# A delta-rule scan and a gated MLP on one core: another order of pieces and lags with fewer idle products, and 64-row products of two neighbouring first-layer tiles in the two halves of the array

## The chip, the core and the metric

The program runs on one core of a Trainium2 chip. Its time is the device time of one execution in microseconds (us); several executions are taken and their median counts. Engines are named as in the profile: PE (TensorE, products), PEld (its weight loads), DVE (VectorE), ACT (ScalarE), POOL (GpSimd) and SP (the engine that issues the transfers).

## The reference

Two parts follow each other. The first is a recurrence over 768 steps for 4 batches x 8 heads with a state of 40x40; the second is a gated MLP with spatial gating on the 4 x 768 x 320 array that the first part leaves.

```python
for t in range(S):                      # S = 768, D = 40
    y[:, :, t] = einsum('bhd,bhde->bhe', rt, state)
    Sa = einsum('bhde,bhe->bhd', state, at)
    state = state * wt[:, :, None, :] - einsum('bhd,bhe->bhde', Sa, bt) + einsum('bhd,bhe->bhde', vt, kt)

h = gelu(x @ w_in)                      # x: 4 x 768 x 320, w_in: 320 x 1024, tanh form
u, v = h[..., :512], h[..., 512:]
v_n = (v - mean) / sqrt(var + 1e-6) * g_ln
v_s = einsum('ts,bsd->btd', w_sg, v_n) + b_sg[None, :, None]    # w_sg: 768 x 768
out = x + (u * v_s) @ w_out             # w_out: 512 x 320
```

All is float32. The large products are made of rounded halves: a value is split into a rounded high part and a rounded rest (names ending in h and l), and a product of two values is high x high, high x low and low x high.

## The kernel before

**The scan.** The 768 steps are 12 chunks of 64. For each chunk DVE builds the gates, PE makes the products ab inside the chunk, ACT copies their blocks out (nts, kbt), POOL inverts a triangular block by pairs of steps tg and x, and PE carries the state from chunk to chunk (ru, sp, ut, pq, yp in the trace). ACT also fills the constant zeros of the tiles rt, vut and xt at the start, by copies from a zeroed tile warm. The results go to DRAM through xd and come back as the rows of x (xt).

**The MLP.** The work of a batch is cut into pieces. x0 and x1 split the two halves of x into the tiles xh and xl (split_x, line 1084). v0 to v5 are the v half of the first layer for 128 rows each (in_v, line 1114; trace name hv, 8 products of 512 columns). u0 to u7 are the u half, transposed, 128 columns by 384 rows each (in_u, line 1142; hu, 8 products of 384 columns). s0 to s7 are the gating product with w_sg (sg, 18 products: 6 chunks of 128 rows times 3 of high and low), o0 to o5 the last layer (op). A batch's first layer has a depth of 320: two chunks of 128 rows and a third of 64. The 64-row tail of x is loaded twice, into both halves of a 128-row tile. In xh[:, 2] the upper half holds the high part and the lower half the rest, so that one 128-row product with the high weights wih[:, 2] does for both; in the product with the low weights wil[:, 2] only the 64 rows of the high part are wanted.

**Order.** The order of the pieces is a table: SEQ0 for batch 0 with batch 1's first layer between (line 93), SEQ for later batches (line 91), SEQL for the last one. run (line 1281) goes through it; before each piece it issues the weight preparation that is due there (loads, splits of w_sg at positions SGS into wsh and wsl, splits of w_out at OUTS; SGE and OUTE say which engine subtracts, V for DVE and G for POOL). Behind each piece product (line 1096) puts the piece's ACT, DVE and POOL steps on a list with a lag in pieces (later), and tick issues what is due: for a v piece p, q, q, v, the statistics bs and mv, the root rs on POOL, and the split into vh (ACT) and vl (POOL). The first five pieces of batch 0 (FILL) run inside the scan.

The scan's order is set by tables of due times and lags too (CH, GPOS, LAG and others); a list JUNK of (due time, count) puts idle products of 512 columns on PE, whose results nobody reads, and a piece "j6" is six of them. All instructions of an engine run in the order in which the program issues them; every row of the trace names line 157, the helper that records them, and so the pieces are told by their tiles.

Of the kernel before, what the change touches and what calls it, by code (L numbers as in the profile page):

```python
# [35 lines left out]
EW = 1.24  # L36
WARM = (14, 0)
T0 = 7.27
T1 = 16.98
T2 = 3.25  # L40
TX = 17.74
LX = 2.88
YM = 64
HEAT = ((13.17, 11),)
LV = 7.67
C1 = 15.05
WP = 16.2
W16 = 0.27
K16 = 0
TB0 = 1.08  # L50
TB1 = 14.03
CUT0 = (2,)
HALF = 9
ROWS0 = (0, 26)
T3 = 11.21
T4 = 15.34
CH = ((0.45, 2.04, 5.42, 6.21, 1.13, 7.18, 8.59, 11.36, 3.3, 10.06, 13.31, 14.77), (0.21, 1.37, 6.72, 4.0, 8.34,
    5.6, 9.88, 10.86, 3.24, 6.16, 13.32, 13.76))
GPOS = (((0.01, 0.33, 0.61, 1.31, 3.87, 4.25, 4.26, 4.27, 0.611), (2.52, 2.51, 2.79, 3.49, 5.81, 6.43, 6.44, 6.45,
# [5 lines left out]
GE = ("VVVVV", "VVV", "V", "V")  # L65
START = (13.53, 0.06)
E0A = "GGGG"
E0K = "GVGG"
E1A = "GGGG"
E1K = "GGGV"  # L70
BACK = (17.21, 22.21, 30.49, 23.63)
GX = (24.18, 3.53)
CG = 0.7978845608028654
G1 = 0.044715
ENDS = {(9, 1): (("g", 0.01),), (10, 1): (("r", 0.01),), (11, 0): (("i", 5.0),)}
PIN = 266.02
DSTEP = ((-13.06, -3.36, 0.0, 0.13, 3.41, 3.62), (-16.79, -1.11, 0.0, 0.61, 3.02, 3.47))
DEC = ((275.89, 0), (276.24, 0), (284.23, 0), (286.85, 0), (290.7, 1), (297.59, 1), (298.13, 1), (306.35, 0),
    (309.82, 0), (317.07, 1), (323.45, 0), (329.7, 1))
PX = 266.05  # L80
PV = 294.03
PL = 335.9
FILL = (("x0", 0, 319.86), ("v0", 0, 331.35), ("v1", 0, 344.98), ("v2", 0, 346.14), ("u0", 0, 349.9))
AFTER = {"v": (0.56, 0.57, 1.47, 1.57, 2.13, 2.48, 2.96, 4.17, 5.19), "u": (1.14, 1.97, 2.82, 3.17), "x": ()}
PX1 = 0
EARLY = 4
PSG = 313.1
SGD = (-6.74, -0.32, 1.37)
SGA = ()
VRING = 10  # L90
SEQ = ("x0", "s1", "x1", "s2", "s0", "s3", "s4", "v0", "s5", "v1", "o0", "o1", "o2", "s6", "s7", "v2", "u0", "v3",
    "u1", "v4", "v5", "o3", "o5", "o4", "u2", "u3", "u4", "u5", "u7", "u6")
SEQ0 = (("x0", 0), ("v0", 0), ("v1", 0), ("v2", 0), ("u0", 0), ("u3", 0), ("x1", 0), ("u1", 0), ("u2", 0), ("v3",
# [4 lines left out]
XL = 4  # L98
REST = 9
SGS = (3, 6, 4, 5, 11, 10, 10, 13, 13, 13, 14, 14)  # L100
OUTS = (11, 12, 12, 14, 15, 18, 19, 18)
XE = "VVVVVVVVVVVV"
UE = "VVVVVVVV"
OSTEP = (-3, -1, 0, 0, 0, 0)
SGE = "GGGGGVGVVVVV"
OUTE = "VVGGGGGG"
SECOND = (17.86, 0.35)
ZERO = (-1, 12.11)
LAST = 2
IS = 1  # L110
NS = 0
PQ = 1
MK = 40
JUNK = ((294.28, 5), (295.93, 4), (307.25, 6), (312.36, 3), (312.43, 1), (346.91, 3), (349.9, 4))
TP = 1
UT = 0
GL = (0.53, 0.99)
LAG = ((0.48, 1.44, 5.43, 0.01, 4.92, 1.62, (0.04, 0.48, 0.01, 1.02), (1.56, 1.57, 0.55, 1.09), 1.82, 0.23, 0.77,
    0.11), (0.2, 0.01, 3.21, 0.78, 1.1, 0.64, (0.26, 0.27, 0.89, 0.9), (0.01, 0.02, 2.06, 2.07), 0.01, 3.4, 0.06,
    0.01))  # L120
# [50 lines left out]
def attention(tc, a, xd, flag, keep, ps, mlp=None):  # L171
# [4 lines left out]
    with ExitStack() as ctx:  # L176
# [643 lines left out]
        def both(c, n, at, w, nm="tv"):  # L820
# [64 lines left out]
class Mlp:  # L885
# [198 lines left out]
    def split_x(self, b, n):  # L1084
        t, h, l = self.xts[b % 2, n], self.xh, self.xl
        self.xin[n] = b
        c = slice(384 * n, 384 * n + 384)
        for k in range(2):
            self.split(h[:, k, c], l[:, k, c], t[:, k], self.A, self.pick(XE, 6 * b + 3 * n + k))
        self.A.copy(out=h[:, 2, c], in_=t[:, 2])  # L1090
        self.pick(XE, 6 * b + 3 * n + 2).tensor_tensor(out=h[64:128, 2, c], in0=t[64:128, 2], in1=h[64:128, 2, c].bitcast(F32), op=ALU.subtract)

    def pick(self, s, k):
        return self.G if k < len(s) and s[k] == "G" else self.V

    def product(self, ops, *steps):
        for i, (o, l, r) in enumerate(ops):
            self.T.matmul(o, lhsT=l, rhs=r, start=(i == 0), stop=(i == len(ops) - 1), skip_group_check=True)
        if self.hold is not None:
            self.hold += [f for _, _, f in sorted(steps, key=lambda x: x[:2])]  # L1100
            return
        self.later(*steps)
        self.tick()
# [10 lines left out]
    def in_v(self, b, tt):  # L1114
        V, G, sb = self.V, self.G, self.pv
        xh, xl, wih, wil = self.xh, self.xl, self.wih, self.wil
        c, f = slice(128 * tt, 128 * tt + 128), slice(HF, DF)
        ops = [(xh[:, k, c], x[:, k, f]) for x in (wih, wil) for k in range(3)]
# [12 lines left out]
        def halves():  # L1131
            h, l = pair
            self.split(h, l, v)
            self.vn[b, tt] = h, l

        self.product([(o, *x) for x in ops], *self.gelu2(o, HF, v),
                     (1, 7, lambda: V.bn_stats(out=bs, in_=v)), (1, 8, lambda: V.bn_aggr(out=mv, in_=bs)), (1, 9, root),
                     (2, 7.5, lambda: V.tensor_scalar(out=v, in0=v, scalar1=mv[:, 0:1], scalar2=rs,
                                                    op0=ALU.subtract, op1=ALU.mult)),
                     (2, 10, halves))  # L1140

    def in_u(self, b, f, n):
# [138 lines left out]
    def run(self, ahead, verdict=None):  # L1281

        done = [(x, b) for x, b, _ in FILL] if ahead else []
        seq, jobs = [], []
# [12 lines left out]
        seq = [x for x in seq if x[1] < B and x not in done and (ahead or x[0][0] != "j")]  # L1297
# [134 lines left out]
```

## Time and profile before

| what | us |
|---|---|
| runs of the kernel before | 619.60, 621.16, 621.56 |
| median | 621.16 |
| the profiled execution | 620.27 |
| its span, first to last instruction | 618.5 |
| PE busy | 578.4 (94%) |
| DVE, ACT, POOL busy | 487.2, 390.9, 374.3 |

The profiled execution is one execution; its span leaves out 1.8 us around the first and last instruction. Mean granted clock of TensorE over the span: 0.945 of full speed. Busy shares are averages over stages that have little in common, the scan up to about 350 us and the MLP after it.

### The profile page before, as it was taken

What the parts mean: (1) busy time and instruction counts of PE and PEld (TensorE: products, weight loads), DVE (VectorE), ACT (ScalarE), POOL (GpSimd) and SP (SyncE); (2) the same over time, 40 slices, a digit from 0 to 9 for tenths busy, and PEclk for the clock granted to TensorE, in tenths of its full rate; (3) what the DMA queues carried; (4) which work ended last, traced back from release to release, by engine and by line L of the source; (5) the groups of instructions that cost most, each with busy time, mean ns of one, the idle gap of its engine ahead of it and who ended that gap; (6) DMA issues with size and microseconds to landing.
All of it is one profiled execution on the core that took longest, in us unless ns stands there. A gap on an engine that the chain in (4) does not pass through costs nothing.

```text
span 618.5 us, 24511 instructions
## 1 busy us (share of the span) xinstructions
PE 578.4 (94%) x10060; PEld 520.8 (84%) x10060; DVE 487.2 (79%) x1085; ACT 390.9 (63%) x1113; POOL 374.3 (61%) x842
## 2 busy tenths in 40 slices
PE   5758999999999999999979999699999999999996
PEld 5557888888888888888868789699899989999995
DVE  7867798988889897798787988898887779568732
ACT  6938798988979889788764856544544256224410
POOL 7768688888888888888886425445533332343230
PEclk9555899999999999999989999899999999999999
DMA  6513243454434543433433424420111103010002
GB/s 207 168 41 89 76 123 104 121 129 117 113 106 117 132 120 104 116 100 92 140 92 100 129 78 141 141 65 10 33 55 54 34 1 108 1 34 13 20 1 70
DMA packets 56889, 54.06 MB, mean 87 GB/s; under 512 B 35840, under 2 KB 47360, under 8 KB 56768
## 3 DMA queue, kind: packets, MB, share of 16 engines
q1 hardware_dynamic: 56768, 52.40, 29.9%
q8 instruction: 81, 1.33, 0.9%
q14 instruction: 40, 0.33, 0.2%
HBM read 44.52 MB, written 7.86 MB: 85 GB/s over the span
## 4 chain that ended last, share of the span: by engine, by line
PE 50%; DVE 15%; ACT 14%; POOL 9%; issue 6%; DMA 4%; SPq 1%; POOLq 0%; ACTq 0%; DVEq 0%
PE sg L157 13%; PE op L157 6%; PE hu L157 6%; PE hv L157 6%; POOL x L157 5%; POOL tg L157 4%; PE ab L157 4%; ACT nts L157 3%; PE sp L157 3%; PE yp L157 3%; PE ru L157 2%; DVE at L157 2%; DMA main<-main 2%; DVE sc L157 2%; DVE ex L157 2%
## 5 line engine op out<-in xcount | busy, mean ns | idle before, releaser
L157 POOL TENSOR_TENSOR tg<-x,n 128x126 f32<-128x126 f32 (+24 forms) x334 | 123.1, 369 | 34.2 <-ACT x L157 5.5
L157 POOL TENSOR_TENSOR x<-x,tg 128x126 f32<-128x126 f32 (+24 forms) x334 | 126.3, 378 | 26.1
L157 PE MATMUL sg<-wsh,vh 128*128 128x384 f32 x192 | 66.0, 344 | 5.7 <-ACT wsh L157 4.5
L157 POOL TENSOR_TENSOR gx<-g,gy 128x384 fp32r<-128x384 f32 x30 | 31.7, 1061 | 64.6 <-ACT gy L157 64.6
L157 PE MATMUL sg<-wsl,vh 128*128 128x384 f32 x192 | 65.7, 342 | 0.4 <-POOL wsl L157 0.4
L157 PE MATMUL sg<-wsh,vl 128*128 128x384 f32 x192 | 65.7, 342 | 0.0
L157 ACT ACTIVATE nts<-ab 32x256 f32<-32x256 f32 x192 | 62.0, 323 | 5.7 <-DVE at L157 3.1
L157 PE MATMUL pq<-rt,vut 128*64 128x128 f32 x768 | 52.9, 281 | 0.0
L157 ACT CAST gy<-g 128x384 fp32r<-128x384 f32 x30 | 15.4, 514 | 55.5 <-DVE g L157 52.2
L157 PE MATMUL ab<-at,kb 64*64 64x64 f32 x1536 | 38.5, 242 | 11.0 <-POOL kb L157 5.4
L157 ACT CAST vh<-v 128x512 fp32r<-128x512 f32 x24 | 14.9, 621 | 51.6 <-DVE v L157 51.6
L157 PE MATMUL yp<-pqs,kbt 128*64 128x64 f32 x768 | 46.5, 225 | 1.0 <-ACT kbt L157 0.4
L157 PEld LDWEIGHTS ab<-at,kb 64*64 64x64 f32 x1536 | 31.7, 150 | 16.6 <-POOL kb L157 6.0
L157 POOL TENSOR_TENSOR vl<-v,vh 128x512 fp32r<-128x512 f32 x24 | 31.6, 1317 | 20.9 <-ACT vh L157 20.9
L157 PEld LDWEIGHTS pq<-rt,vut 128*64 128x64 f32 x768 | 41.8, 139 | 2.3 <-issue 0.7
L157 PEld LDWEIGHTS sg<-wsh,vh 128*128 128x128 f32 x192 | 36.9, 192 | 6.6 <-ACT wsh L157 4.8
L157 PE MATMUL yp<-rt,s 80*40 80x64 f32 x704 | 42.3, 219 | 0.0
L157 PEld LDWEIGHTS yp<-pqs,kbt 128*64 128x64 f32 x768 | 37.1, 136 | 5.4 <-DVE sc L157 2.2
L157 DVE SCALAR_TENSOR_TENSOR g<-sg,gl,bt 128x384 f32<-128x384 f32 x32 | 19.7, 615 | 25.4 <-PE sg L157 24.4
L157 DVE TENSOR_TENSOR at<-ab,mask 64x256 f32<-64x256 f32 x96 | 35.7, 407 | 4.5 <-PE ab L157 3.9
L157 PEld LDWEIGHTS sg<-wsl,vh 128*128 128x128 f32 x192 | 36.9, 192 | 1.0 <-POOL wsl L157 0.8
L157 PE MATMUL ru<-rhsb,xt 64*64 64x40 f32 x768 | 32.2, 234 | 5.7 <-ACT xt L157 5.3
(166 smaller groups left out, 1652.7 us busy)
## 6 DMA issues: line engine op xcount, KB each, us to landing
main<-main SPq DMA_DIRECT2D x88, 160.8 KB
vs<-vb SPq DMA_DIRECT2D x24, 160.0 KB
vu<-vs SPq DMA_DIRECT2D x24, 160.0 KB
rt<-rt SPq DMA_DIRECT2D x48, 80.0 KB
vut<-vt SPq DMA_DIRECT2D x24, 160.0 KB
xd<-yt SPq DMA_DIRECT2D x96, 40.0 KB
xt<-xd SPq DMA_DIRECT2D x16, 192.0 KB
out<-y SPq DMA_DIRECT2D x16, 192.0 KB
```

Of the source, the lines that this page charges most:

```text
L157: return self.tc.keep_in_program_order(f(*a, **k))
```

## The change

Four things are changed.

1. The product with the 64 useful rows becomes the last of a v or u piece. Where two u or v pieces are neighbours in the table, the first piece leaves it out, and behind the second piece's other products both follow as 64-row products: the first piece's on rows 0 to 63 of xh, the second's on rows 64 to 127 of a new tile xb, which holds the high part there. The follow-up steps of both pieces are then issued one after the other. A u or v piece without such a neighbour keeps its 128-row product. There are 23 such pairs (10 of two u pieces, 6 of two v, 7 of one each); 6 pieces of the tables stay alone, and so do those inside the scan. For xb, split_x makes two ACT casts of 64 rows out of one of 128. EARLY gives one pair of v tiles less to the scan's time, which makes room for xb.
2. The idle products in JUNK go from 26 to 13 and those in pieces from 6 (j6) to 5 (j2, j3).
3. The order of pieces: batch 0 now has u1 u2, v5 v4, v3 u5, u4, j2, u7 u6, s1; later batches have v0 and v1 side by side. One w_sg split is two positions earlier, one is subtracted on DVE instead of POOL, and pieces of w_out move.
4. The scan's due times and lags. On PE the scan's order stays as it was but for the idle products; on ACT copies of constants change place at the start.

```diff
-T1 = 16.98
+T1 = 17.63
...
-EARLY = 4
+EARLY = 3
...
-SEQ = ("x0", "s1", "x1", "s2", "s0", "s3", "s4", "v0", "s5", "v1", "o0", "o1", "o2", "s6", "s7", "v2", "u0", "v3",
+SEQ = ("x0", "s1", "x1", "s2", "s0", "s3", "s4", "v0", "v1", "s5", "o0", "o1", "o2", "s6", "s7", "v2", "u0", "v3",
...
-SGS = (3, 6, 4, 5, 11, 10, 10, 13, 13, 13, 14, 14)
+SGS = (3, 6, 4, 5, 11, 10, 10, 11, 13, 13, 14, 14)
-SGE = "GGGGGVGVVVVV"
+SGE = "GGGVGVGVVVVV"
...
-JUNK = ((294.28, 5), (295.93, 4), (307.25, 6), (312.36, 3), (312.43, 1), (346.91, 3), (349.9, 4))
+JUNK = ((296.7, 4), (299.18, 4), (312.36, 3), (314.34, 2))
...
+        self.pair, self.first = 0, None
...
+        self.xb = p.tile([128, S], F32R, name="xb")
...
     def split_x(self, b, n):
...
-        self.A.copy(out=h[:, 2, c], in_=t[:, 2])
-        self.pick(XE, 6 * b + 3 * n + 2).tensor_tensor(out=h[64:128, 2, c], in0=t[64:128, 2], in1=h[64:128, 2, c].bitcast(F32), op=ALU.subtract)
+        z = self.xb[64:128, c]
+        self.A.copy(out=z, in_=t[64:128, 2])
+        self.A.copy(out=h[0:64, 2, c], in_=t[0:64, 2])
+        self.pick(XE, 6 * b + 3 * n + 2).tensor_tensor(out=h[64:128, 2, c], in0=t[64:128, 2], in1=z.bitcast(F32), op=ALU.subtract)
...
-    def product(self, ops, *steps):
-        for i, (o, l, r) in enumerate(ops):
-            self.T.matmul(o, lhsT=l, rhs=r, start=(i == 0), stop=(i == len(ops) - 1), skip_group_check=True)
+    def product(self, ops, *steps, third=None):
+        ops = [(*x, not i, i == len(ops) - 1 and not third) for i, x in enumerate(ops)]
+        if third and not self.pair:
+            ops.append((*third(slice(0, 128)), False, True))
+        if third and self.pair == 2:
+            for k, f in enumerate((self.first[0], third)):
+                ops.append((*f(slice(64 * k, 64 * k + 64)), False, True))
+        for o, l, r, start, stop in ops:
+            self.T.matmul(o, lhsT=l, rhs=r, start=start, stop=stop, skip_group_check=True)
+        if third and self.pair == 1:
+            self.first = third, steps
+            return
+        if third and self.pair == 2:
+            self.later(*self.first[1])
+            self.tick()
...
     def in_u(self, b, f, n):
...
-        ops = [(x[:, k, fc], xh[:, k, c]) for x in (wih, wil) for k in range(3)]
+        ops = [(x[:, k, fc], xh[:, k, c]) for x in (wih, wil) for k in range(3 if x is wih else 2)]
...
-        self.product([(o, *x) for x in ops], *self.gelu2(o, 384, u))
+
+        def third(r):
+            return o, wil[r, 2, fc], (self.xb[r, c] if r.start else xh[r, 2, c])
+
+        self.product([(o, *x) for x in ops], *self.gelu2(o, 384, u), third=third)
...
     def run(self, ahead, verdict=None):
...
+            if self.pair == 1:
+                self.pair = 2
+            else:
+                self.pair = int(x[0] in "uv" and i + 1 < len(seq) and seq[i + 1][0][0] in "uv")
             self.piece(x, b)
```

The remaining lines of the diff are other numbers of these tables, and in_v has the same edit as in_u.

**PE, from the last u pieces of batch 0 to the start of s1** (hu and hv are the first layer's products, xl and wil low parts, idle the idle products, sg the gating product). Before:

```order
L157 MATMUL hu<-xh,wih 128x384 x3
L157 MATMUL hu<-xh,wil 128x384 x3
L157 MATMUL hu<-xl,wih 128x384 x2
L157 MATMUL hu<-xh,wih 128x384 x3
L157 MATMUL hu<-xh,wil 128x384 x3
L157 MATMUL hu<-xl,wih 128x384 x2
L157 MATMUL idle<-wih 128x512 x6
L157 MATMUL sg<-wsh,vh_7684 128x384
```

and now, from the end of the piece u4:

```order
L157 MATMUL hu<-xh,wil 128x384
L157 MATMUL idle<-wih 128x512 x2
L157 MATMUL hu<-xh,wih 128x384 x3
L157 MATMUL hu<-xh,wil 128x384 x2
L157 MATMUL hu<-xl,wih 128x384 x2
L157 MATMUL hu<-xh,wih 128x384 x3
L157 MATMUL hu<-xh,wil 128x384 x2
L157 MATMUL hu<-xl,wih 128x384 x2
L157 MATMUL hu<-xh,wil 128x384
L157 MATMUL hu<-xb,wil 128x384
L157 MATMUL sg<-wsh,vh_7699 128x384
```

The six idle products are gone, two stand further ahead, and the two last products of u7 and u6, the second on xb, follow each other at the end.

**ACT at the start of the program**, up to and behind the copy into x that the first inverse works on (nts and kbt copy blocks of ab; rt, vut and at are filled with constants or copied; junk sums a row of inputs). Before:

```order
L157 ACTIVATE nts_101<-ab_369 32x256
L157 ACTIVATE nts_101<-ab_369 32x4x32
L157 COPY rt_132<-warm 128x1024
L157 ACTIVATE junk,wsum<-main_94 128x256
L157 COPY kbt_107<-ab_368 128x160
L157 COPY kbt_107<-ab_369 128x160
L157 COPY at_165<-at_165 64x4x64
L157 ACTIVATE junk,wsum<-main_95 128x256
L157 COPY x<-x_140 128x512
L157 ACTIVATE nts_102<-ab_422 32x256
```

and now:

```order
L157 ACTIVATE nts_101<-ab_368 32x4x32
L157 ACTIVATE junk,wsum<-main_94 128x256
L157 COPY kbt_107<-ab_367 128x160
L157 COPY kbt_107<-ab_368 128x160
L157 COPY at_165<-at_165 64x4x64
L157 ACTIVATE junk,wsum<-main_95 128x256
L157 COPY x<-x_140 128x512
L157 ACTIVATE nts_102<-ab_420 32x256
L157 ACTIVATE nts_102<-ab_420 32x4x32
L157 ACTIVATE nts_102<-ab_421 32x256
L157 ACTIVATE nts_102<-ab_421 32x4x32
L157 COPY rt_132<-warm 128x1024
```

The copy of zeros into the second rt has moved from ahead of the copy into x to behind the next four nts. The copy into the first rt, further up, has moved behind the nts of the third chunk of gates and stays ahead of x.

**ACT ahead of the stop of s1 in batch 0** (vh is the cast of the batch's last v piece, wsh are casts of w_sg, p and q the gelu steps of u pieces, sc a step of a w_out split). Before:

```order
L157 CAST vh_8536<-v 128x512
L157 ACTIVATE p<-hu 128x384
L157 ACTIVATE q<-q 128x384
L157 CAST wsh<-ws 128x384 x2
L157 ACTIVATE sc<-stg 128x256
L157 ACTIVATE p<-hu 128x384
L157 ACTIVATE q<-q 128x384
L157 CAST wsh<-ws 128x384
```

and now:

```order
L157 CAST vh_8523<-v 128x512
L157 CAST wsh<-ws 128x384 x4
L157 ACTIVATE sc<-stg 128x256 x2
L157 ACTIVATE p<-hu 128x384
L157 ACTIVATE q<-q 128x384
L157 ACTIVATE p<-hu 128x384
L157 ACTIVATE q<-q 128x384
```

Four wsh casts stand in a row behind vh; before, two stood there and a third behind a sc, a p and a q. The steps p and q of u7 and u6 have moved behind them.

## Rows read from the trace of the kernel before

**Rows 1.** The page: busy us, share of the span and instructions.

```profile
PE 578.4 (94%) x10060; PEld 520.8 (84%) x10060; DVE 487.2 (79%) x1085; ACT 390.9 (63%) x1113; POOL 374.3 (61%) x842
```

**Rows 2.** Stretches: us, then busy us (instructions) per engine, clock, DMA share, GB/s.

```profile
core 0: us, PE busy (x) PEld busy (x) DVE busy (x) ACT busy (x) POOL busy (x), PEclk, DMA share, GB/s
14.60:66.00 51.40, 38.13 (x901) 33.32 (x902) 39.54 (x102) 38.24 (x115) 37.01 (x113) 0.50 0.36 102
...
318.00:326.00 8.00, 7.29 (x106) 6.70 (x106) 6.57 (x16) 5.02 (x14) 6.90 (x15) 0.57 0.58 146
...
393.00:405.00 12.00, 7.09 (x25) 6.69 (x25) 10.55 (x29) 6.21 (x16) 3.68 (x4) 0.72 0.41 115
...
434.70:601.70 167.00, 166.97 (x918) 160.85 (x919) 119.75 (x240) 66.42 (x134) 58.89 (x61) 1.00 0.11 33
```

**Rows 3.** Chain that ended last, 300 to 440 us: start, us, what.

```profile
by line: POOL x L157 10.5%; POOL tg L157 9.6%; issue 7.4%; PE hv L157 7.3%; DVE sc L157 6.4%; PE hu L157 5.1%; PE yp L157 4.4%; DVE g L157 4.4%; PE pq L157 3.5%; DVE lt L157 2.6%; DVE stg L157 2.5%; PE sg L157 2.4%; DMA stg<-w 2.3%; DVE v L
...
328.30 0.46 POOL x L157
...
358.19 2.04 PE hv L157 x8
...
368.76 0.68 PE idle L157 x3
...
370.51 1.12 PE idle L157 x4
371.63 1.39 PE hu L157 x8
...
374.10 4.39 PE hu L157 x24
378.48 3.68 PE hv L157 x16
```

**Rows 4.** Timeline of POOL: start, us, instruction, idle before it and releaser.

```profile
24.98 0.21 POOL L157 TENSOR_TENSOR tg<-x,n 128x15 f32<-128x15 f32 x1 [2.23 <-ACT x L157]
```

**Rows 5.** Timeline of PE, in s1 of batch 0.

```profile
397.53 0.69 PE L157 MATMUL sg<-wsh,vh 128*128 128x384 f32 x1 [4.52 <-ACT wsh L157]
...
399.09 0.52 PE L157 MATMUL sg<-wsh,vl 128*128 128x384 f32 x1
399.41 0.52 PE L157 MATMUL sg<-wsh,vh 128*128 128x384 f32 x1
```

**Rows 6.** PE groups by form, 66 to 300 us: count, busy us, mean ns.

```profile
L157 PE MATMUL ab<-at,kb 64*64 64x64 f32 x1152 | 25.5, 224 | 0.0
...
L157 PE MATMUL ab<-ident,kb 104*128 104x104 f32 x144 | 20.7, 266 | 0.0
```

**Rows 7.** Timeline of PE, in o2 of batch 0.

```profile
432.15 0.51 PE L157 MATMUL op<-gx,woh 128*64 128x384 f32 x2
432.50 0.33 PE L157 MATMUL op<-gy,woh 128*128 128x384 f32 x1
```

**Rows 8.** Timeline of PE, the start of s7 of batch 0.

```profile
434.73 0.45 PE L157 MATMUL sg<-wsh,vh 128*128 128x384 f32 x1 [1.20 <-DVE v L157]
```

**Rows 9.** Timeline of ACT, before the stop in s1.

```profile
393.71 0.62 ACT L157 CAST vh<-v 128x512 fp32r<-128x512 f32 x1 [1.13 <-DVE v L157]
...
395.03 0.91 ACT L157 CAST wsh<-ws 128x384 fp32r<-128x384 f32 x2
...
396.96 0.51 ACT L157 CAST wsh<-ws 128x384 fp32r<-128x384 f32 x1
```

**Rows 10.** Timeline of ACT at the start of the program.

```profile
21.46 1.05 ACT L157 COPY rt<-warm 128x1024 f32<-128x1024 f32 x1
...
24.30 0.60 ACT L157 COPY x<-x 128x512 f32<-128x512 f32 x1
```

**Rows 11.** Timeline of PE, idle products near the end of the scan.

```profile
327.95 1.43 PE L157 MATMUL idle<-wih 128*128 128x512 f32 x5
...
338.69 1.65 PE L157 MATMUL idle<-wih 128*128 128x512 f32 x6
```

**Rows 12.** Timeline of POOL, before the stop in s1.

```profile
394.41 1.27 POOL L157 TENSOR_TENSOR vl<-v,vh 128x512 fp32r<-128x512 f32 x1 [1.06 <-ACT vh L157]
...
397.55 0.99 POOL L157 TENSOR_TENSOR wsl<-ws,wsh 128x384 fp32r<-128x384 f32 x1 [0.46 <-ACT wsh L157]
```

More of the change, by code (lines that the diff above doesn't have):

```diff
@@ L38 @@
 T0 = 7.27
-T1 = 16.98
+T1 = 17.63
 T2 = 3.25
-TX = 17.74
-LX = 2.88
+TX = 17.76
+LX = 3.25
 YM = 64
[L44 to L48, printed above, removed]
+HEAT = ((12.88, 11),)
+LV = 8.05
+C1 = 15.63
+WP = 16.1
+W16 = 0.54
 K16 = 0
-TB0 = 1.08
-TB1 = 14.03
+TB0 = 1.03
+TB1 = 14.64
 CUT0 = (2,)
[L53 to L58, printed above, removed]
+HALF = 5
+ROWS0 = (16, 31)
+T3 = 10.02
+T4 = 16.93
+CH = ((-0.19, 2.04, 5.23, 6.38, 1.0, 7.53, 8.59, 11.41, 3.24, 9.89, 13.23, 14.77), (-0.81, 1.36, 7.03, 4.55, 8.4,
+    5.62, 9.88, 10.69, 3.24, 5.87, 13.53, 13.76))
 GPOS = (((0.01, 0.33, 0.61, 1.31, 3.87, 4.25, 4.26, 4.27, 0.611), (2.52, 2.51, 2.79, 3.49, 5.81, 6.43, 6.44, 6.45,
@@ L64 @@
     0.01, 0.55, 1.95, 8.6, 11.86, 11.87, 12.06, 0.551),))
-GE = ("VVVVV", "VVV", "V", "V")
-START = (13.53, 0.06)
+GE = ("VVVVG", "VVV", "V", "V")
+START = (13.59, 3.46)
 E0A = "GGGG"
@@ L70 @@
 E1K = "GGGV"
-BACK = (17.21, 22.21, 30.49, 23.63)
-GX = (24.18, 3.53)
+BACK = (17.21, 19.94, 29.98, 23.52)
+GX = (24.18, 3.29)
 CG = 0.7978845608028654
@@ L76 @@
 PIN = 266.02
-DSTEP = ((-13.06, -3.36, 0.0, 0.13, 3.41, 3.62), (-16.79, -1.11, 0.0, 0.61, 3.02, 3.47))
-DEC = ((275.89, 0), (276.24, 0), (284.23, 0), (286.85, 0), (290.7, 1), (297.59, 1), (298.13, 1), (306.35, 0),
-    (309.82, 0), (317.07, 1), (323.45, 0), (329.7, 1))
+DSTEP = ((-14.04, -3.61, 0.0, 0.13, 3.21, 3.62), (-16.79, -0.16, 0.0, 1.16, 3.02, 3.47))
+DEC = ((275.89, 0), (276.24, 0), (284.23, 0), (286.85, 0), (292.17, 1), (297.59, 1), (298.13, 1), (306.35, 0),
+    (309.82, 0), (317.07, 1), (323.66, 0), (329.7, 1))
 PX = 266.05
@@ L82 @@
 PL = 335.9
-FILL = (("x0", 0, 319.86), ("v0", 0, 331.35), ("v1", 0, 344.98), ("v2", 0, 346.14), ("u0", 0, 349.9))
-AFTER = {"v": (0.56, 0.57, 1.47, 1.57, 2.13, 2.48, 2.96, 4.17, 5.19), "u": (1.14, 1.97, 2.82, 3.17), "x": ()}
+FILL = (("x0", 0, 319.88), ("v0", 0, 331.76), ("v1", 0, 344.98), ("v2", 0, 346.14), ("u0", 0, 349.9))
+AFTER = {"v": (0.56, 0.57, 1.47, 1.57, 2.13, 2.32, 2.8, 4.01, 5.03), "u": (1.14, 1.97, 2.99, 3.34), "x": ()}
 PX1 = 0
-EARLY = 4
+EARLY = 3
 PSG = 313.1
-SGD = (-6.74, -0.32, 1.37)
+SGD = (-4.57, -1.67, 0.36)
 SGA = ()
 VRING = 10
-SEQ = ("x0", "s1", "x1", "s2", "s0", "s3", "s4", "v0", "s5", "v1", "o0", "o1", "o2", "s6", "s7", "v2", "u0", "v3",
+SEQ = ("x0", "s1", "x1", "s2", "s0", "s3", "s4", "v0", "v1", "s5", "o0", "o1", "o2", "s6", "s7", "v2", "u0", "v3",
     "u1", "v4", "v5", "o3", "o5", "o4", "u2", "u3", "u4", "u5", "u7", "u6")
-SEQ0 = (("x0", 0), ("v0", 0), ("v1", 0), ("v2", 0), ("u0", 0), ("u3", 0), ("x1", 0), ("u1", 0), ("u2", 0), ("v3",
[4 rows of a table removed]
+SEQ0 = (("x0", 0), ("v0", 0), ("v1", 0), ("v2", 0), ("u0", 0), ("u3", 0), ("x1", 0), ("u1", 0), ("u2", 0), ("v5",
[4 rows of a table added]
 XL = 4
 REST = 9
-SGS = (3, 6, 4, 5, 11, 10, 10, 13, 13, 13, 14, 14)
-OUTS = (11, 12, 12, 14, 15, 18, 19, 18)
+SGS = (3, 6, 4, 5, 11, 10, 10, 11, 13, 13, 14, 14)
+OUTS = (14, 12, 12, 14, 15, 18, 19, 16)
 XE = "VVVVVVVVVVVV"
@@ L104 @@
 OSTEP = (-3, -1, 0, 0, 0, 0)
-SGE = "GGGGGVGVVVVV"
-OUTE = "VVGGGGGG"
+SGE = "GGGVGVGVVVVV"
+OUTE = "VVGGVGGG"
 SECOND = (17.86, 0.35)
-ZERO = (-1, 12.11)
+ZERO = (-1, 15.71)
 LAST = 2
@@ L113 @@
 MK = 40
-JUNK = ((294.28, 5), (295.93, 4), (307.25, 6), (312.36, 3), (312.43, 1), (346.91, 3), (349.9, 4))
+JUNK = ((296.7, 4), (299.18, 4), (312.36, 3), (314.34, 2))
 TP = 1
 UT = 0
[L117 to L120, printed above, removed]
+GL = (0.01, 0.01)
+LAG = ((0.99, 0.01, 0.51, 0.01, 0.01, 1.74, (0.01, 0.84, 0.72, 1.39), (2.06, 2.6, 0.59, 0.7), 1.86, 0.36, 0.55,
+    0.01), (1.1, 0.2, 4.43, 0.65, 1.29, 1.35, (0.01, 0.28, 0.48, 0.49), (1.05, 1.46, 2.06, 2.07), 0.01, 1.74, 0.01,
+    0.21))
 SEQL = ("s1", "s2", "s0", "s3", "s4", "s5", "s6", "s7", "o0", "o1", "o2", "o3", "o5", "o4")
@@ L1117, in in_v @@
         c, f = slice(128 * tt, 128 * tt + 128), slice(HF, DF)
-        ops = [(xh[:, k, c], x[:, k, f]) for x in (wih, wil) for k in range(3)]
+        ops = [(xh[:, k, c], x[:, k, f]) for x in (wih, wil) for k in range(3 if x is wih else 2)]
         ops += [(xl[:, k, c], wih[:, k, f]) for k in (0, 1)]
@@ L1134, in halves @@
             self.vn[b, tt] = h, l
+        def third(r):
+            return o, (self.xb[r, c] if r.start else xh[r, 2, c]), wil[r, 2, f]
         self.product([(o, *x) for x in ops], *self.gelu2(o, HF, v),
@@ L1139, in in_v @@
                                                     op0=ALU.subtract, op1=ALU.mult)),
-                     (2, 10, halves))
+                     (2, 10, halves), third=third)
     def in_u(self, b, f, n):
@@ L1149, in in_u, with third @@
         u = self.us[b, f, n] = self.ut.pop((f, n))
-        self.product([(o, *x) for x in ops], *self.gelu2(o, 384, u))
+        def third(r):
+            return o, wil[r, 2, fc], (self.xb[r, c] if r.start else xh[r, 2, c])
+        self.product([(o, *x) for x in ops], *self.gelu2(o, 384, u), third=third)
     def sgu(self, b, f, n):
```

8 rows, old and new, of the table SEQ0 are left out of this document.

## The prediction

> **What bounds the kernel now.** I read the page's busy rows and its chain first, then the table of stretches, then single instructions. On the page PE is busy 94% of the span [rows 1], but that is an average over stages with different limits. From 14.6 to 66 us the granted clock is 0.50, so 1.2 GHz [rows 2]. In the later chunks of the scan POOL's inverse steps tg and x follow one another and set the pace: in the chain from 300 to 440 they come first of all lines, with 9.6 and 10.5% [rows 3], and all of that lies before 329. The first inverse starts at 24.98 us, released by an ACT copy into x [rows 4]. From 350 us PE is the bound: the chain runs through hv, hu, yp and idle products without a break until 382 [rows 3], and from 434.70 to 601.70 PE is busy 166.97 of 167.00 us [rows 2]. Between them lies one hole: s1 of batch 0 stops at its fifth weight chunk for 4.52 us on ACT's wsh, and afterwards 17 products come every 0.32 us [rows 5], against the 0.174 of a product of the same width below; the stretch from 393 to 405 has a clock of 0.72 [rows 2].
>
> The profiled execution took 620.27 us (span 618.5); the median of the runs is 621.16, 0.9 more. All sums are made against 620.27, and 0.3% (1.9 us) is what I take as no change.
>
> **Pairs, the 64-row products.** An hv or hu piece is 8 products; the last now has 64 useful rows, and in 23 pairs two such products stand next to each other in opposite row halves. If they run at the same time a pair saves one product: a dense hu piece takes 1.39 us for 8, 0.174 each, and 16 hv products take 3.68, 0.230 each [rows 3]. Four pairs (two hu-hu, hv-hv, hv-hu) stand ahead of the hole at 393, where PE then only waits longer, so I count them at nothing by themselves; the wait covers them, and if it vanished they would give 0.7 more. Of the other 19, 8 are hu-hu and 6 mixed (the shorter one is hidden: 14 x 0.174 = 2.4) and 5 hv-hv (5 x 0.230 = 1.15): **-3.6 us**, all in the stretch where PE has no idle time.
> Whether the halves run together this trace shows only for smaller tiles: 1152 ab products on 64x64 tiles were busy 25.5 us, 22 ns each for 64 columns, while 144 products on one 104x128 tile took 20.7 us, 144 ns each for 104 columns [rows 6]. Scaled by columns (144 x 64/104 = 89) that is four at a time; two column halves alone would give 44 ns, so row halves do overlap. This is the lower end, -3.6. The upper end is a loss: coming back from the small tiles of pq and yp to whole products, 8 hv products take 2.04 instead of 1.84 and 24 hu products 4.39 instead of 3 x 1.39 [rows 3], 0.20 to 0.22 us per return. Between them stands the nearest row: o2 alternates whole products and 128x64 ones, of the same rounded type as hu and hv, and two 128x64 ones between whole ones take 0.35 us from start to start, no longer than whole ones [rows 7]. I take that row, since it is nearest in type and place, and charge no switch. Weight loads are the second doubt: PEld is busy 160.85 of the 167 us [rows 2], and two halves need two loads in the time of one product. If loads set the pace the saving is 0; that is a rival below.
> The Trainium skill, page "TensorEngine Tiling (Array Packing)", section "Key Properties", says that a change of tiling mode drains TensorE. It speaks against this change, which changes mode twice per pair. The 0.20 us returns agree with it, o2 does not; by the rule the pairs would cost time instead of giving it (rival two).
>
> **The first piece of a pair** keeps its bank and starts its ACT and DVE work one piece later, 1.4 to 1.8 us. In the dense stretch DVE works 119.75 of 167 us, ACT and POOL less [rows 2], and five to ten other pieces stand between a u or v and its reader. I cost it at nothing; without that cover PE would wait as at 434.73, 1.20 us for DVE to release a bank [rows 8], once per batch at most, so 0 to +3.6.
>
> **split_x** casts a half twice: one more ACT instruction per x piece, 8 in all, about as long as a whole cast (0.51 us for wsh [rows 9]). ACT is busy 66.42 of 167 us there: nothing; 0 to +0.5.
>
> **The start.** Two copies of zeros into rt (1.05 us each) stood on ACT ahead of the copy into x that releases the first inverse. The first one stays ahead of it, the second, at 21.46, now follows it [rows 10]. What remains ahead follows with hardly a gap, so x comes 1.05 earlier, less an estimated 0.1 for what the moved first copy and the small xt copy delay: POOL waited 2.23 us for it [rows 4], so it follows. From there the chain goes through half-clocked PE work and POOL's inverses to 349.67: **-0.9**. Ends: -1.05, and 0 if something else in the first chunks is late next, a gate of DVE's or a half-clocked product.
>
> **Idle products.** x3 (0.68 us) and x4 (1.12 us) at 368.76 and 370.51 lay on the chain [rows 3] and are gone: -1.8 ahead of the hole. x5 and x6 at 327.95 and 338.69 [rows 11] stand where the chain is POOL's inverse and what DVE and ACT make of it; the new x4 between the two halves of ru and x5 instead of x4 after xp, before 347, stand there too: nothing, and up to +1.1 if that x4 ends last. New j3 ahead of o1 adds 3 x 0.23 = 0.7 us of PE ahead of the 1.20 us wait at 434.73 [rows 8]; since POOL and DVE steps of w_out move too, I charge **+0.3** (0 to +0.7).
>
> **The hole at 393.** PE arriving earlier only waits longer; what counts is when the fifth chunk's wsh and wsl are there. The third v of the batch now leaves ACT earlier because x3 and x4 and two products are gone in front of it, but its last product comes only with u5's: -1.6 - 0.4 + 1.2 = -0.8 on PE; DVE and ACT steps behind it stay the same, with one wsl more on DVE. Behind the vh cast (393.71 + 0.62 = 394.33) the wanted wsh was the third of three, behind p, q, two casts, sc, p and q, at 396.96 [rows 9]. Now it is the third of four casts in a row, at 0.91 - 0.51 = 0.40 us each: 394.33 + 0.80 = 395.13. POOL though has vl until 394.41 + 1.27 = 395.68 and another wsl of some 1.0 to 1.1 us first [rows 12]: the wanted wsl starts at about 396.9 instead of 397.55. So -0.65 from the order and -0.8 to -1.6 from in front: I take **-1.9** for the restart; ends -0.6 and -2.6. The half-speed products behind it (17 x 0.147 = 2.5 us) I leave, for the hole stays about as long: the six products j6 in front of it are gone too.
>
> **Sum:** -3.6 - 0.9 + 0.3 - 1.9 = -6.1; 620.27 - 6.1 = **614.2 us**.
>
> **Rivals.**
> 1. *The halves run one behind the other, or weight loads set the pace.* The pairs save nothing: 617.8. For it: the load row of rows 2. Against it: the ab rows [rows 6]. Chance 0.14.
> 2. *Slower: every switch between whole array and halves costs what the returns from pq and yp show.* Two per pair at 0.21 us are 0.42, against 0.19 saved: 19 x 0.23 = +4.4 in place of -3.6, so 620.27 + 4.4 - 0.9 + 0.3 - 1.9 = 622.2. It decides from where a switch costs over 0.16 us: then 19 x (0.32 - 0.19) = 2.5 takes up all the other gains. For it: the 0.20 and 0.22 us of the returns; against it: o2 [rows 7]. The skill's drain of the page above is this rival. Chance 0.12.
> 3. *The clock.* 14 idle products fewer. The stretch from 318 to 326 had a mean clock of 0.57 [rows 2]; one more such stretch on the chain costs 8 x 0.43 = 3.4 us: 617.6. The gaps near 330 and 339, where x5 and x6 stood, are the place. Against it: they are short, 1.43 and 1.65 us [rows 11]. Chance 0.10.
> 4. *The other way:* the hole becomes so short that the clock stays up: 2.5 less, 611.7. Chance 0.09.
>
> **How the numbers follow.** The forecast has 0.55. It and rival 4 are faster by over 0.3%; of rivals 1 and 3, which lie 0.4% below, I count 0.15 as faster and 0.09 as the same; rival 2 is slower with 0.10, else the same. Faster 0.78, the same 0.12, slower 0.10. The range goes from 611.0 (the hole ends early) to 620.5, which takes in rivals 1 and 3 with a late bank or two and leaves out rival 2 and the far ends.
>
> **What would show it.** Right: a paired piece's last two products start within some 30 ns of each other and the next whole product 0.17 to 0.23 us later; a stretch from s7 of batch 0 to the last op about 3.4 us shorter than 167; the first POOL inverse near 24.0; the s1 stop ending near 396.7. Wrong: a gap of 0.2 us behind each pair, halves 0.17 apart, clock below 1.00 in 328 to 350, or new PE waits for DVE within the dense stretch.

## The result and the profile after

The changed kernel is slower: median 626.2 us (four executions, 623.87 to 626.92) against 621.36 us of the kernel before (four, 619.6 to 621.72), a ratio of 1.0084 with a 95% interval of 1.006 to 1.0109. Its profiled execution, the fastest of the four, took 623.87 us with a span of 622.1, 3.6 more than before in both. I had 614.2 with a range to 620.5.

The busy row of the page, against [rows 1]:

```profile
PE 578.4 (93%) x10046; PEld 511.2 (82%) x10046; DVE 491.3 (79%) x1088; ACT 397.1 (64%) x1121; POOL 374.7 (60%) x839
```

PE is busy as long as before, to the tenth, although 14 idle products and 23 products' worth of pairs should be missing; PEld, the weight loads, is 9.6 us shorter. So something may take PE time without being a product of its own; busy time also depends on the granted clock, so this is only a hint. The place is found by following one instruction of the program through both traces:

| instruction | before | after | difference |
|---|---|---|---|
| first inverse step tg on POOL | 24.98 | 24.41 | -0.57 |
| last inverse step tg on POOL | 332.10 | 331.64 | -0.46 |
| third vh cast on ACT (v2 of batch 0) | 374.18 | 373.67 | -0.51 |
| fourth vh cast | 387.70 | 387.84 | +0.14 |
| 19th sg product, behind the stop in s1 | 400.37 | 400.19 | -0.18 |
| first sg product of s7 of batch 0 | 434.73 | 434.86 | +0.13 |
| last sg product | 601.34 | 605.04 | +3.70 |

Up to s7 nothing is won or lost; the whole loss lies in the stretch from s7 to the last sg product, 166.61 us before and 170.18 now, where PE is the bound and 18 of the 23 pairs stand (one more stands between the stop and s7, four ahead of the stop). One of them, the timeline of PE in the kernel after (start, us, instruction):

```profile
458.88 0.51 PE L157 MATMUL hu<-xl,wih 128*128 128x384 f32 x2
459.32 0.44 PE L157 MATMUL hu<-xh,wil 64*128 64x384 f32 x1
459.32 0.44 PE L157 MATMUL hu<-xb,wil 64*128 64x384 f32 x1
459.69 0.44 PE L157 MATMUL sg<-wsh,vh 128*128 128x384 f32 x1
459.97 0.34 PE L157 MATMUL sg<-wsl,vh 128*128 128x384 f32 x1
```

The two 64-row products (64*128, on xh and on xb) start in the same hundredth of a microsecond: they do run together. But of the two xl products ahead of them the second begins at 458.88 + 0.17 = 459.05, so the next slot would be 459.22; the halves begin 0.10 later. The next whole product comes 0.37 us after them instead of 0.17, and the one behind it after 0.28. Lost are 0.10 + 0.20 + 0.11 = 0.4 us, saved is one product. PE's weight loads, PEld, show where:

```profile
459.32 0.18 PEld L157 LDWEIGHTS hu<-xh,wil 64*128 64x128 f32 x1 [0.25 <-issue]
459.32 0.18 PEld L157 LDWEIGHTS hu<-xb,wil 64*128 64x128 f32 x1
459.69 0.19 PEld L157 LDWEIGHTS sg<-wsh,vh 128*128 128x128 f32 x1 [0.18 <-issue]
459.80 0.19 PEld L157 LDWEIGHTS sg<-wsl,vh 128*128 128x128 f32 x1
```

Between whole products a load runs a product ahead of its own matmul (459.80 for the product at 459.97). At both borders of the pair it does not: PEld stands still for 0.25 and 0.18 us, and load and matmul then begin together, at 459.32 and at 459.69. The Trainium skill, page "TensorEngine Tiling (Array Packing)", section "Key Properties", says that a change of tiling mode drains TensorE. This trace agrees for row halves: the loads wait at both borders. What it costs, these rows give.

The other half of the story is the stop in s1. Timeline of PE after, against [rows 5]:

```profile
394.52 0.69 PE L157 MATMUL sg<-wsh,vh 128*128 128x384 f32 x1 [3.27 <-ACT vh L157]
...
398.42 0.69 PE L157 MATMUL sg<-wsl,vh 128*128 128x384 f32 x1 [1.54 <-POOL wsl L157]
398.91 0.52 PE L157 MATMUL sg<-wsh,vl 128*128 128x384 f32 x1
399.23 0.52 PE L157 MATMUL sg<-wsh,vh 128*128 128x384 f32 x1
```

PE now stops behind nine sg products instead of twelve. It restarts at 394.52, 3.0 us earlier than before, on the vh of the last v piece, and then waits 1.54 us for POOL's wsl. The 15th product starts at 398.91, 0.18 earlier than before (399.09), and the products behind it come every 0.32 us again. ACT and POOL in the same place, against [rows 9] and [rows 12]:

```profile
393.85 0.62 ACT L157 CAST vh<-v 128x512 fp32r<-128x512 f32 x1 [1.13 <-DVE v L157]
394.37 1.75 ACT L157 CAST wsh<-ws 128x384 fp32r<-128x384 f32 x4
```

```profile
394.54 1.28 POOL L157 TENSOR_TENSOR vl<-v,vh 128x512 fp32r<-128x512 f32 x1 [1.07 <-ACT vh L157]
395.77 2.59 POOL L157 TENSOR_TENSOR wsl<-ws,wsh 128x384 fp32r<-128x384 f32 x2
```

```profile
394.91 2.60 DVE L157 TENSOR_TENSOR wsl<-ws,wsh 128x384 fp32r<-128x384 f32 x2 [0.56 <-ACT wsh L157]
```

The four wsh casts are in a row, as the order said, the vh ahead of them is no earlier (393.85, before 393.71), and POOL's two wsl take 2.59 us, 1.30 each against 1.07 and 0.99 before. At the same time DVE does two wsl of its own, also 1.30 each.

### The profile page after: what moved, and what is told of

It reads as the page before. It is cut to its first block, busy times and chain, and to the rows that moved or that the text cites. A ratio compares the mean times of both kernels' runs of the same rounds, so it can differ in the third digit from the quotient of the medians.

```text
span 622.1 us, 24494 instructions
## 1 busy us (share of the span) xinstructions
PE 578.4 (93%) x10046; PEld 511.2 (82%) x10046; DVE 491.3 (79%) x1088; ACT 397.1 (64%) x1121; POOL 374.7 (60%) x839
## 4 chain that ended last, share of the span: by engine, by line
PE 46%; DVE 16%; ACT 14%; POOL 9%; issue 7%; DMA 5%; SPq 1%; DVEq 0%; POOLq 0%; ACTq 0%
PE sg L157 13%; PE op L157 7%; PE hv L157 6%; PE hu L157 5%; POOL x L157 4%; ACT nts L157 4%; POOL tg L157 4%; PE ab L157 3%; PE yp L157 3%; DVE at L157 2%; DMA main<-main 2%; PE sp L157 2%; PE ru L157 2%; DVE ex L157 2%; ACT junk L157 2%
## 5 line engine op out<-in xcount | busy, mean ns | idle before, releaser
L157 POOL TENSOR_TENSOR x<-x,tg 128x126 f32<-128x126 f32 (+24 forms) x334 | 129.1, 387 | 26.0
L157 POOL TENSOR_TENSOR tg<-x,n 128x126 f32<-128x126 f32 (+24 forms) x334 | 121.3, 363 | 31.8 <-DVE n L157 4.2
L157 POOL TENSOR_TENSOR rs<-rs,mhalf 128x1 f32<-128x1 f32 x24 | 13.4, 559 | 50.6 <-DVE rs L157 46.1
L157 PEld LDWEIGHTS sg<-wsh,vl 128*128 128x128 f32 x192 | 37.0, 193 | 0.9 <-POOL vl L157 0.9
```

Of the source, the lines that this page charges most:

```text
L157: return self.tc.keep_in_program_order(f(*a, **k))
```

## The experiments

All were timed beside the kernel before on the same chip. The stretch from the first sg product of s7 of batch 0 to the last sg product is read from each trace as above; it does not depend on what happened earlier. Before it is 166.61 us, after 170.18. "Per pair" divides by the pairs that stand in it (18; in the old order 16).

**No pairs.** Every u and v piece keeps its 128-row product.

```diff
-                self.pair = int(x[0] in "uv" and i + 1 < len(seq) and seq[i + 1][0][0] in "uv")
+                self.pair = 0
```

> The changed kernel with its pairs switched off: every u and v piece keeps its 128-row product as its last, all else (order, lags, idle products) as changed. From the first product of s7 of batch 0 to the last sg product the kernel before took 166.6 us and the changed one 170.2. Theory A (each switch of TensorE between whole array and halves costs, about 0.39 us per pair against 0.17 to 0.23 saved): the stretch falls to about 166.6 and the whole time by 3.5 to 4.5 us against the changed kernel, to about 620 to 622. Theory C (the new order of pieces loses the time): the stretch stays near 170 and the time near 624 to 626.

Measured: 621.37 us, ratio 1.0005 (0.9978 to 1.0032). First and last sg product of the stretch:

```profile
436.27 0.34 PE L157 MATMUL sg<-wsh,vh 128*128 128x384 f32 x1
...
602.73 0.34 PE L157 MATMUL sg<-wsh,vl 128*128 128x384 f32 x1
```

That is 166.46 us: the loss is the pairs', not the new order's (theory A, not C). It also says that all the rest of the change together is worth nothing that can be measured: the interval reaches from 1.4 us faster to 2.0 slower, and I had 2.5 faster.

**Whole pairs.** The pairs stay, with the late follow-up of the first piece, but both last products have 128 rows.

```diff
-                ops.append((*f(slice(64 * k, 64 * k + 64)), False, True))
+                ops.append((*f(slice(0, 128)), False, True))
```

> The changed kernel, pairs kept in place (both last products behind the second piece, both pieces' follow-up steps late), but both products whole, 128 rows. Theory A (the switch costs): stretch from s7 of batch 0 to the last sg product near 166.6 us, as without pairs. Theory B (the late follow-up of the first piece and its bank held longer cost the time): the stretch stays near 170 us, with PE waits in it.

Measured: 622.17 us, ratio 1.0026 (0.999 to 1.0062); stretch 435.40 to 602.00, 166.60 us, no PE wait over 0.04 us in it. Theory A holds; the late follow-up costs nothing in this stretch. Ahead of the stop in s1 it does: from the third to the fourth vh cast this kernel takes 13.85 us, the one without pairs 13.05, the changed one 14.17. So the pairs cost 1.1 us there, 0.8 of it by the late follow-up and 0.3 by the switches, and the stop waits for the vh that come behind it. From the last vh cast to the 19th sg product the late follow-up costs another 0.3: 6.34 us with whole pairs, as in the changed kernel, and 6.02 without pairs.

**Same half.** Both products of a pair on rows 0 to 63.

```diff
-                ops.append((*f(slice(64 * k, 64 * k + 64)), False, True))
+                ops.append((*f(slice(0, 64)), False, True))
```

> The changed kernel, but both 64-row products of a pair on rows 0 to 63, so that they can't run together. Theory A (halves do run together, the switch eats more than they give): each of the 19 pairs in the stretch takes a product more, 0.17 to 0.23 us, so the stretch goes from 170.2 to about 173.8 us. Theory D (halves run one behind the other, or their weight loads set the pace): no change, about 170.2 us.

Measured: 631.02 us, ratio 1.017 (1.0119 to 1.0221). The two ends of the stretch, and a pair in it:

```profile
437.80 0.34 PE L157 MATMUL sg<-wsh,vh 128*128 128x384 f32 x1
...
453.50 0.51 PE L157 MATMUL hu<-xl,wih 128*128 128x384 f32 x2
453.94 0.62 PE L157 MATMUL hu<-xh,wil 64*128 64x384 f32 x2
454.48 0.79 PE L157 MATMUL hu<-xh,wih 128*128 128x384 f32 x3
...
611.35 0.34 PE L157 MATMUL sg<-wsh,vl 128*128 128x384 f32 x1
```

173.55 us, against 173.8 by theory A and 170.2 by theory D. Serial halves cost 6.94 / 18 = 0.39 us per pair more than two whole products: that is the price of the visit by itself (from whole products into the halves and back), since nothing is saved. In the pair above it is spread over four steps, each some 0.1 us longer than the 0.17 of whole products: 0.27 to the first half, 0.28 to the second, 0.26 and 0.28 to the two whole products behind. A pair saves 0.19 on average in this stretch (8 pairs hu-hu and 5 mixed at 0.174, 5 hv-hv at 0.230), and the changed kernel's own loss is 3.57 / 18 = 0.20: 0.39 - 0.19. Both give the same price.

**Four halves.** In each pair the product with the second chunk of low weights is made a 64-row product too, in the piece's own half; the other 64 rows of that chunk are left out of the sum.

```diff
-            for k, f in enumerate((self.first[0], third)):
-                ops.append((*f(slice(64 * k, 64 * k + 64)), False, True))
+            for n in (1, 2):
+                for k, f in enumerate((self.first[0], third)):
+                    ops.append((*f(slice(64 * k, 64 * k + 64), n), False, n == 2))
...
```

> The changed kernel, and in each pair the product with the second chunk of low weights is also made a 64-row one in the piece's half (the other 64 rows of that chunk's low weights are left out of the sum). So each pair has two whole products less and four halves in place of two. Theory A with the cost per switch of mode: the stretch falls by one product per pair, from 170.2 to about 166.6 us. Theory E (the cost comes with each half product, by its weight load, not with the switch): each further pair of halves costs what the first did, so the stretch stays above 168.5 us.

Measured: 620.81 us, ratio 1.0016 (0.9988 to 1.0043); stretch 433.98 to 601.13, 167.15 us. Theory A said 166.6, theory E above 168.5. Saved are (170.18 - 167.15) / 18 = 0.17 us per visit against the changed kernel: a second pair of halves behind the first takes the time of one product and no further price. The price belongs to the visit, not to the half products. With two products saved per visit it is about even: (167.15 - 166.61) / 18 = 0.03 us lost. With one it loses 0.20.

**Old order with pairs.** The tables of the kernel before (but EARLY 3), the new product, split_x and run.

```diff
-        for i, (o, l, r) in enumerate(ops):
-            self.T.matmul(o, lhsT=l, rhs=r, start=(i == 0), stop=(i == len(ops) - 1), skip_group_check=True)
+        ops = [(*x, not i, i == len(ops) - 1 and not third) for i, x in enumerate(ops)]
...
```

> The kernel before with the pairs alone: its own order, lags and idle products, and the new product and split_x; 21 pairs, 17 of them behind the stop in s1. (EARLY is 3 as in the change, to make room for xb.) Theory A (a pair nets a loss of about 0.19 us, whatever the order): the stretch from s7 of batch 0 to the last sg product goes from 166.6 us to about 169.8, the time from 620.5 to about 624. Theory C (it is the new order in which pairs fall badly): 166 or less.

Measured: 625.64 us, ratio 1.0078 (1.0054 to 1.0102); stretch 436.27 to 606.18, 169.91 us, 3.30 / 16 = 0.21 per pair: the net loss is the same in the old order.

**Columns.** The same pairs, but each product has all 128 rows and 64 weight columns (the third low chunk of the other 64 columns is left out).

```diff
-                ops.append((*f(slice(64 * k, 64 * k + 64)), False, True))
+                o, l, r = f(slice(0, 128))
+                ops.append((o[slice(0, 64)], l[:, slice(0, 64)], r, False, True))
```

> The changed kernel with the two 64-row products of each pair made into two products of all 128 rows and 64 weight columns, out on partitions 0 to 63 (as op's 128x64 products in o2; the third low chunk of the other 64 columns is left out). It asks why o2's row did not show the price. Theory A1 (a tile of half the rows means a switch, one of 64 columns does not): the stretch from s7 of batch 0 to the last sg product is 166.6 us, as with whole products. Theory A2 (every smaller tile means a switch, and o2 was an exception): 166.6 + 18 x 0.39 = 173.6 us, as with both products in the same half of the rows.

Measured: 622.13 us, ratio 1.0005 (0.9971 to 1.0039). The pair that stood above at 459.32, here:

```profile
463.09 0.51 PE L157 MATMUL hu<-xl,wih 128*128 128x384 f32 x2
463.43 0.51 PE L157 MATMUL hu<-xh,wil 128*64 128x384 f32 x2
463.78 0.34 PE L157 MATMUL sg<-wsh,vh 128*128 128x384 f32 x1
463.95 0.34 PE L157 MATMUL sg<-wsl,vh 128*128 128x384 f32 x1
```

```profile
463.26 0.30 PEld L157 LDWEIGHTS hu<-xh,wil 128*64 128x64 f32 x2
463.60 0.19 PEld L157 LDWEIGHTS sg<-wsh,vh 128*128 128x128 f32 x1
```

Two products in 0.35 us, the next loads ahead of their matmuls, no gap; stretch 439.46 to 606.17, 166.71 us. Theory A1: 64 columns with their output on partitions 0 to 63 cost no switch, 64 rows do. Columns of the other half were not tried.

**Idle kept.** No pairs, and x5 and x6 back at their places near 328 and 339 us.

```diff
-JUNK = ((296.7, 4), (299.18, 4), (312.36, 3), (314.34, 2))
+JUNK = ((294.28, 5), (296.7, 4), (299.18, 4), (307.25, 6), (312.36, 3), (314.34, 2))
...
```

> The changed kernel without pairs, and with the idle products x5 and x6 of the kernel before put back at their two places near 328 and 339 us. Theory F (without them PE has gaps there, the granted clock falls between 336 and 350 us and the gain of the start is lost): the clock of 336 to 350 is 1.00 as before, against 0.59 to 0.79 in three of the runs without them, and the time is 1 to 3 us below that without pairs (621.4), about 619. Theory G (PE follows DVE there anyway, the clock costs nothing): no difference, about 621.

Measured: 622.12 us, ratio 1.0021 (0.9998 to 1.0044). The stretch around it, without and with the two (us, busy us of PE, PEld, DVE, ACT, POOL, granted clock, DMA share, GB/s):

```profile
332.00:352.00 20.00, 17.76 (x359) 15.06 (x361) 15.75 (x38) 11.46 (x31) 6.84 (x9) 0.74 0.40 112
```

```profile
332.00:352.00 20.00, 19.96 (x439) 16.23 (x434) 16.25 (x39) 12.96 (x37) 9.35 (x16) 1.00 0.37 105
```

Theory F is half right. The clock does fall without them: it was below 1.00 from 332 to 352 in five of the six traces without x5 and x6 and 1.00 in all five with them. In the two with 0.74 (no pairs, columns) the way from the last inverse step to the first vh took 3.0 and 2.8 us longer than before; in the others, the changed kernel's with 0.91 among them, under 0.8. But the time came out no better with them, 622.1 against 621.4: theory G as far as the median goes.

**Less idle.** The kernel before without x3 and x4.

```diff
-JUNK = ((294.28, 5), (295.93, 4), (307.25, 6), (312.36, 3), (312.43, 1), (346.91, 3), (349.9, 4))
+JUNK = ((294.28, 5), (295.93, 4), (307.25, 6), (312.36, 3), (312.43, 1))
```

> The kernel before without the idle products x3 and x4 near 368 and 370 us (seven products, 1.8 us on the chain of waits), nothing else changed. My prediction's step: PE reaches s1 1.8 us earlier, and the stop there ends earlier by as much as its wsh and wsl do, so 0.6 to 1.8 us less in all, about 619. Theory H (the v chain on DVE and ACT and the wsl subtraction on POOL set the end of the stop, not PE): PE reaches s1 1.8 us earlier and waits 1 us or more longer, time 620 to 620.5.

Measured: 620.43 us, ratio 0.9993 (0.9975 to 1.0011). 1.8 us of products are taken off PE's chain and 0.5 us is won from the third to the fourth vh (12.97 us against 13.52), since PE now waits for the split of x1, which DVE does.

```profile
379.48 0.50 PE L157 MATMUL hv<-wih,xh 128*128 128x512 f32 x1 [0.76 <-DVE xh L157]
```

The times do not separate the two theories (the interval reaches from 1.6 us faster to 0.7 slower); the trace does. Only 0.5 of the 1.8 us arrives, as theory H has it, but in another way: PE's own arrival at s1 is 0.5 us earlier relative to the third vh, and it waits there as long as before (4.51 us, before 4.52).

**Fifth first.** No pairs, x5 and x6 kept, and the fifth w_sg chunk cast and subtracted first behind the last vh, with one subtraction less on DVE there.

```diff
-SGS = (3, 6, 4, 5, 11, 10, 10, 11, 13, 13, 14, 14)
+SGS = (3, 6, 4, 5, 10, 10, 10, 13, 13, 13, 14, 14)
-SGE = "GGGVGVGVVVVV"
+SGE = "GGGGGVGVVVVV"
...
```

> A version meant to beat both: no pairs, x5 and x6 kept, the changed order otherwise, and the fifth chunk of w_sg cast first behind the third vh (not third), its subtraction first on POOL, with one subtraction less on DVE at that time. Theory H: the stop in s1 ends about 1.1 us or more earlier than without pairs; the time is 1 to 2 us below idle_kept, about 617 to 618.

Measured: 621.68 us, ratio 1.0019 (1.0 to 1.0038): it beats neither. The stop does end earlier: from the last vh cast (394.59) to the 19th sg product (399.66) it takes 5.07 us, against 6.02 without pairs (395.27 to 401.29) and 6.66 before. That is 0.95 us less than without pairs, where 1.1 or more was expected. Part of it is lost again on the way to s7:

```profile
427.35 0.44 PE L157 MATMUL op<-gx,woh 128*128 128x384 f32 x1 [0.46 <-POOL gx L157]
...
433.74 0.44 PE L157 MATMUL op<-gy,woh 128*128 128x384 f32 x1 [0.56 <-DVE g L157]
```

The second wait, for DVE's g, stands without pairs too (0.60 us there); the first, 0.46 us for POOL's gx, is new. From the third vh to s7 this kernel takes 59.70 us, 60.06 without pairs and 60.55 before, so that 0.36 of the 0.95 us arrives at s7. That s7 starts at 435.25, later than before, is due to the stages ahead of the third vh (375.55, before 374.18).

## Why the prediction was wrong

- **The pairs, -3.6 us: wrong in size and in sign; this step decides the result.** I took the o2 row [rows 7] as nearest and "charge no switch". Measured: +3.6 us in the stretch from s7 on, 0.39 us per visit against 0.19 saved. This is rival two: priced from the returns out of pq and yp [rows 3], 0.21 us per switch, it had 0.42 per pair; the halves measured 0.39. That 0.42 and 0.39 lie so close is partly luck: the way in cost 0.1 and the way back 0.3, not 0.21 each. The mistake was the choice between two rows. I judged nearness by the type of the data and by the place, and did not ask what sets the rows apart. Their form does not: pq's tiles are 128*64 like o2's and keep all rows. The loads do. Before, at a return out of pq:

```profile
357.09 1.09 PE L157 MATMUL pq<-rt,vut 128*64 128x128 f32 x16
358.12 0.96 PE L157 MATMUL hv<-wih,xh 128*128 128x512 f32 x3
```

```profile
358.12 0.53 PEld L157 LDWEIGHTS hv<-wih,xh 128*128 128x128 f32 x3 [0.17 <-issue]
```

PEld stands still for 0.17 us, and then load and product begin together, as at the borders of a pair. Around the 128x64 products of the columns experiment, in the very place of the pairs, loads run ahead and nothing is lost. pq writes output partitions 0 to 63 and 64 to 127 in turn (line 705 of the kernel), o2 and columns only 0 to 63; pq is also plain float32 and not rounded. Which of the two makes pq's return cost is open. That the halves run together, read from [rows 6], was right.
- **The first piece's late follow-up, at nothing:** right where I argued it (the dense stretch: 166.60 us in whole pairs, no waits), wrong for batch 0, which I had left out of that argument. There the fourth to sixth vh hang on it and the stop hangs on them: 0.8 us, and 1.1 with the switches of the pairs ahead of it, which I had counted as covered by the wait. Altogether the changed kernel takes 231.4 us from the third vh to the last sg product and the kernel without pairs 226.5: 4.8 us, of which 3.7 are lost in the stretch from s7 on. That agrees with the distance of the two measured ratios, 1.0084 with pairs and 1.0005 without (0.79% or 4.9 us, each ratio to some 0.25%), and in the old order pairs cost 4.9 us over the same way (232.1 against 227.2).
- **The start, -0.9:** the first inverse came 0.57 us earlier in the changed kernel, the direction was right. It does not arrive: at the last inverse step the eight traces with the new start lie from 1.2 us ahead of the kernel before to 1.7 behind (mean 332.5), and the three with the old start from 332.1 to 333.6 (mean 332.6). The clock of the stretch from 30 to 66 us was 0.50 before, 0.64 in the changed kernel and 0.71 without pairs: when it rises differs from execution to execution (what sets the moment is open), and a gain of 0.57 drowns in that. That the changed kernel's trace is still 0.5 ahead at the third vh is luck of this execution: the eight new ones reach it at 375.7 on average, the three old ones at 374.6.
- **The stop, -1.9 on top of the start:** it ended 0.18 us earlier in all, which is 0.33 later when counted from the third vh. My -0.65 from the order of casts came out without pairs (6.02 against 6.66 us from vh to the 19th product), and with them at half (6.34): the late follow-up brings DVE's second wsl ahead of POOL's second one, and POOL's two take 2.59 us instead of 2.27. The part from in front (-0.8 to -1.6) was the failing one: x3 and x4, on the chain as the profile drew it, give 0.5 when taken out, since the split of x1 and the v chain on DVE and ACT are next; and the pairs took 1.1 back.
- **j3, +0.3:** s7 starts without the 1.20 us wait of [rows 8]; the three products and a wait of 0.49 us for DVE's g at 433.36 stand in its room. From the 19th product to s7 the changed kernel takes 0.31 us more, so the step came out in this trace; in the six others with this order of steps it is between 0.0 and 0.6.
- **The clock, rival three:** its mechanism is there, in five traces of six, at the place named. Its price, 3.4 us in the forecast, was nearly paid in two of them (3.0 and 2.8), and not in the changed kernel's own trace. Rival four did not come: the products behind the stop start every 0.32 us as before.

Of the 9.7 us between 614.2 and 623.87, 7.2 are the pairs in the dense stretch (+3.6 in place of -3.6), 2.2 the stop (+0.3 in place of -1.9) and 0.4 the start (-0.5 in place of -0.9). The median, 626.2, lies another 2.3 us above the profiled execution; the other three left no trace, so what they lost is not seen.

## What to carry to other kernels

Before small tiles are packed into a stream of whole products, count what is saved per visit, not per product: a visit to row halves cost 0.39 us here, as much as two products. With one saved product it lost, with two it was about even, and by these figures (an estimate, it was not run) it would pay from three on. When two rows of one trace disagree on what a switch costs, ask what differs between them before taking one. The form of the tiles does not tell it (pq and o2 are both 128*64); the weight loads do: where PEld stands still on "issue" alone and load and product then begin together, a border has been paid for. And work taken off a chain is worth what the second-latest input allows: here 0.5 of 1.8 us.

## What the runs showed of the hardware

- A visit from whole products to 64-row ones costs 0.39 us, whether the other half is used (at 459.32: 0.1 on the way in and 0.3 on the way out) or not (same half: 0.1 at each of four steps); loads do not run ahead over either border. A second pair of halves in the visit adds 0.17 us, the time of one product. 64 weight columns on all rows, output on partitions 0 to 63, cost nothing (166.71 us for the stretch).
- Of two subtractions with two inputs each, one on DVE and one on POOL, the one that starts second is held up. In the stop of the changed kernel each wsl started while a subtraction of the other engine was running, and all four took about 1.3 us. In the kernel before DVE's started while POOL stood still:

```profile
395.69 0.55 DVE L157 TENSOR_TENSOR wsl<-ws,wsh 128x384 fp32r<-128x384 f32 x1
```

0.55 us alone, and POOL's 0.99 [rows 12]. Without pairs POOL's second one started just ahead of DVE's:

```profile
398.48 0.99 POOL L157 TENSOR_TENSOR wsl<-ws,wsh 128x384 fp32r<-128x384 f32 x1
```

```profile
398.51 1.38 DVE L157 TENSOR_TENSOR wsl<-ws,wsh 128x384 fp32r<-128x384 f32 x1
```

POOL lost nothing, DVE 0.83 us. The Trainium skill, page "SBUF — State Buffer", section "Who interferes with whom", says that a VectorE instruction with two SBUF inputs contends with a GpSimd one that reads SBUF, over ports that are an exclusive lock; these traces agree. So a step moved from POOL to DVE beside another such step, as the change does with a chunk of w_sg, moves less than its own length.
- In the eight single traces of kernels with the new first stage, the last inverse step stood 1.2 us ahead to 1.7 us behind the kernel before, and the clock of 30 to 66 us between 0.50 and 0.71: a gain under that size in the first stage can't be told in one trace.
